# Twenty weight folds as ten units of 32x32 TensorE tiles, and two gates moved within the last stage

## The chip, the cores and the metric

The kernel runs on one core of one Trainium2 chip. The metric is the device time of one execution in microseconds (us). The kernel before takes 2380.1 us, the median of three executions that lie between 2378.39 and 2380.84 us.

## What is computed

`x` is 2048 x 1024 float32. It is normalised by rows to `xn`. One branch is linear attention with 32 heads of 32 columns, the other a gated feed-forward layer of width 3584, and the output joins them:

```python
xn = layernorm(x)
q, k, v = heads(xn @ wqkv)                       # 32 heads of 32
pq, pk = q @ w_phi[h], k @ w_phi[h]              # 32x32 per head
phi(p) = concat(softmax(p), softmax(-p))
o = phi(pq) (phi(pk)^T v) / (phi(pq) . sum(phi(pk)) + 1e-6)
s = o @ wo
g = silu((silu(xn @ w1) * (xn @ w3)) @ w2)
out = x + s * g
```

Since `w_phi` acts on each head alone, the kernel folds it into the weights first: a column block of `wk` and of `wq` for one head is multiplied by that head's 32x32 matrix. These products are the folds that the change is about.

## The kernel before

**Stages.** Stage 1 computes `xn @ w1` and `xn @ w3` for 28 feature chunks `f` of 128 and two halves `tb` of the rows; each pair (tb, f) takes seven block products in the order of `ORDER` (names A11, A12, S2, S1, S3, S4, A22; index j = 0 to 6). Stage 2 makes keys, values and queries, stage 3 multiplies by `w2`, stage 4 (the last) does attention's last products and the output by 16 row tiles `t`. A product is written as a high and a low part with three passes (`PASSES`), so that one of the seven is twelve 128x128 by 512 products on TensorE. The entries of `events` are called steps here; step k is one call `gate_up(k)`. Step 52 is (tb 0, f 7, j 3), step 175 is (0, 25, 0) and step 196 begins the second half.

**Order.** In stages 1, 3 and 4 every engine's instructions, and the transfers on SP's queue, stand in the order of the program (`in_order`). Each queue is served in that order: an instruction that waits holds all behind it. In one step the order is: loads of raw weights (`load_at`), what `before` lists, the twelve products, the next split of weights (`prep_at`, four steps ahead of their use: ScalarE casts the high part, line 92, VectorE subtracts the low part, line 93), the sums of a new chunk's raw weights (`sums_at`; lines 128 and 129), what `after` lists, and last the reading of the PSUM bank (`read`).

**What `read` does.** A11 (j 0): ScalarE copies bank b to `h0` (line 625). A12 (j 1): VectorE adds bank a to `h0` (627), ScalarE applies silu (631). S2 (j 2): ScalarE copies bank b to `u0` (633). S1 (j 3): ScalarE copies bank c to `u1` (639). S3, S4 and A22 follow on VectorE and ScalarE (641 to 653). A11, S2, S3 and A22 of a chunk add up in one bank b, so S3's products wait until the copy of line 633 has read what S2 left.

**Side work and its planner.** Other work is put between the steps: turning and splitting rows of `x` (`side_x`), folds (`side_fold`), sums and splits of key and value weights (`side_kv`, eight blocks), stores of operands (`side_store`), and in the second half `side_w`. Each VectorE piece asks `room(step, cost)` for the first step from `step` on whose planned cost stays at or under 2.55. The steps' own costs are in `base`: in steady state 1.22 at j 2, 3, 4 and 5, 1.22 or 1.83 by turns at j 0, and 1.83 at j 1 and 6. A `side_kv` block asks for three pieces of 1.22 (the sums, B11, B21) and five of 0.61 (T2, T1, T3, B22, T4), one after the other; its four raw blocks are loaded five steps ahead of the sums, and each split is stored two steps later (line 444). The pieces are planned in the order of the calls near line 535: `side_x`, `side_fold`, `side_kv`, `side_store`, `side_w`.

**Folds.** Twelve folds are done at the start. Each of the other twenty (`side_fold`) loads 256 KB of `wkT` or `wqT` into a buffer of the pool `xp` (tag x, 14 buffers), multiplies its four 128x128 blocks by block diagonals `bd` of `w_phi` (line 247) into a PSUM bank of tag tr, copies the bank back on ScalarE (line 500) and stores 256 KB (line 501). The folds stand at steps 67 to 171, and ask the planner for nothing.

**Pools.** `xp` (28 KB of each partition) and `bdp` (the 4 KB of `bd`) are closed at step 175, and the pool `spare` takes their 32 KB. At once `fetch` (line 164) issues the loads of two operands of the second half, `op1A11` and `op1A12`, four transfers of 512 KB each, into the two tiles of `spare`. A tile that takes the room of others waits until the last instruction that uses those is done. Splits take buffers of tag q, 11 in all; `h0`, `u0`, `u1` and `t2` take those of tag w, 5 in all. The raw weights of f 27 are loaded at step 178 (lines 256 and 257) and summed at step 183.

**Last stage.** `attend(t, c)` does 32 products in 64x32 tiles (line 1336), read by ScalarE and VectorE (1341, 1342); `out_half` does 24 products of 128x128 by 512 (1351). `gate(i, j)` applies silu to one row tile of the feed-forward output (line 1053). The last pair, i = 7, is row tiles 11 and 15.

Of the kernel before, what the change touches and what calls it, by code (L numbers as in the profile page):

```python
# [8 lines left out]
F = mybir.dt.float32  # L9
# [7 lines left out]
S, D, H, DH, FF = 2048, 1024, 32, 32, 3584  # L17
P = 128
NT = S // P
ND = D // P  # L20
NF = FF // P
G = 8
NKB = NF // 4
FOLDS = 12
# [5 lines left out]
def tile_kernel(ctx: ExitStack, tc: tile.TileContext, x, wkT, wqT, wv, wphi, wo, w1, w3, w2, out):  # L30
    nc = tc.nc
    open_pools = {}

    def pool(name, bufs, **kw):

        open_pools[name] = tc.tile_pool(name=name, bufs=bufs, reuse_waits="tile", **kw)
        return open_pools[name].__enter__()
# [29 lines left out]
    pairs = [(8 * (i // 4) + i % 4, 8 * (i // 4) + i % 4 + 4) for i in range(NT // 2)]  # L67

    dram = ctx.enter_context(tc.tile_pool(name="dram", bufs=1, space=DRAM))
# [3 lines left out]

    xo_d = [{n: dram.tile([P, 4, 2, 4, P], F, name=f"xo_d{tb}{n}") for n in ANAMES} for tb in range(2)]
    wkv_d = [{n: dram.tile([P, 2, 4, 512], F, name=f"wkv_d{c}{n}") for n in BNAMES} for c in range(3)]
    wk_d = [[dram.tile([P, 512], F, name=f"wk_d{c}_{k}") for k in range(ND)] for c in range(2)]
    wq_d = [[dram.tile([P, 512], F, name=f"wq_d{c}_{k}") for k in range(ND)] for c in range(2)]


    wo_d = [[dram.tile([P, 2, 512], F, name=f"wo_d{c}_{k}") for k in range(ND)] for c in range(2)]  # L80
# [63 lines left out]
    ps = pool("ps2", 2, space=PSUM)  # L144
    BANKS = {"a": 1, "b": 2, "c": 2}
# [27 lines left out]
    def blk(name):  # L173
        return xp.tile([P, 4, P], F, name=name, tag="x")

    def flat(t):
        return t.rearrange("p k t -> p (k t)")
# [4 lines left out]
    early_z = small.tile([P, 256 + PAD], F, name="early_z", bufs=1)[:, :256]  # L182
    bd = bdp.tile([P, G, P], F, name="bd")
# [31 lines left out]
    def turn(half):  # L215
        pt = ps.tile([P, 4, P], F, name="pt", tag="tr", bufs=3)
        for k in range(4):
            nc.tensor.transpose(pt[:, k, :], half[:, k * P:(k + 1) * P], ident)
        return pt
# [18 lines left out]
    def load_w(wT, dch, c, t=None):  # L238
        wr = blk("wr") if t is None else t
        nc.sync.dma_start(wr, wT[dch][:, 4 * c:4 * c + 4])  # L240
        return wr

    def fold(wr, c):

        pw = ps.tile([P, 4, P], F, name="pw", tag="tr", bufs=3)
        for g in range(4):
            nc.tensor.matmul(pw[:, g, :], wr[:, g], bd[:, 4 * c + g, :], start=True, stop=True)  # L247
        return pw

    folds = [(wkT, k, c, wk_d[c][k]) for c in range(2) for k in range(ND)]  # L250
    folds += [(wqT, k, c, wq_d[c][k]) for c in range(2) for k in range(ND)]

    def b_load(f):

# [32 lines left out]
        nc.sync.dma_start(r.rearrange("p u n -> p (u n)"), x[t * P:(t + 1) * P, :])  # L287
        xs.append([r[:, h] for h in range(2)])

    phi_raw = flat(blk("phi")[:, :2]).rearrange("p (g f) -> p g f", f=DH)  # L290
    nc.sync.dma_start(phi_raw, wphi)
    fold_rooms = [room_b[:, 4 + k] for k in range(4)]
    fold_rooms += [work.tile([P, 4, P], F, name="wr", tag="h1", bufs=2) for _ in range(2)]
# [19 lines left out]
    for j in range(4):  # L313
        sl = slice(32 * j, 32 * j + 32)
# [57 lines left out]
    before, after, rooms = {}, {}, []  # L372
# [6 lines left out]
    def at(step, f, d=after):  # L379
        d.setdefault(step, []).append(f)  # L380
# [6 lines left out]
    events = [(0, f, j) for f, j in FIRST_PAIR] + [(0, f, j) for f in range(2, NF) for j in range(7)]  # L387
# [40 lines left out]
    def room(step, cost):  # L428

        while base.get(step, 0) + took.get(step, 0) + cost > 2.55:  # L430
            step += 1
        took[step] = took.get(step, 0) + cost
        return step

    def store_quad(step, d, src, name, then=None):

        step = room(step, 2 * OP_US if then else OP_US)

        def f():
            t = qp.tile(list(src().shape[:1]) + [2] + list(src().shape[1:]), R, name=name, tag="q")  # L440
            split(t[:, 0], t[:, 1], src())
            if then:
                then()
            at(step + 2, lambda: nc.sync.dma_start(d, t.bitcast(F)))
        at(step, f)
        return step

    def side_x(i, s0):
        xt, a, mv, sd, pts = [], {}, [], [], {}
        t0, t1 = pairs[i]  # L450

        def load():
            xt.extend(load_x(t, [flat(blk("xt")) for _ in range(2)]) for t in (t0, t1))
            mv.append(small.tile([P, 2, 2], F, name="mv", bufs=4))

        at(s0, load)
        at_ = s0 + 2
        for j in range(2):
            at_ = room(at_ + 1, 1.3)
            at(at_, lambda j=j: stats(mv[0], j, xt[j]))  # L460
        at_ = room(at_ + 1, 1.0)
        at(at_, lambda: sd.append(list(rstd(mv[0]))[1]))
        for j in range(2):
            at_ = room(at_ + 1, 1.0)
            at(at_, lambda j=j: norm(mv[0], sd[0], j, xt[j]))
        s1 = at_ + 1
        for m, (n, j, hf) in enumerate((("A11", 0, 0), ("A12", 0, 1), ("A21", 1, 0), ("A22", 1, 1))):
            at(s1 + m, lambda n=n, j=j, hf=hf: pts.update({n: turn(xt[j][hf])}), before)
            at(s1 + m, lambda n=n: a.update({n: raw_x(pts[n])}))
        at_ = s1  # L470
        for n in ("A11", "A12"):
            at_ = store_quad(at_ + 1, xo_d[1][n][:, i - 4], lambda n=n: a[n], f"xo{n}")
        at_ = max(at_, s1 + 6)
        for m in range(3):
            at_ = room(at_ + 1, OP_US if m else 2 * OP_US)
            at(at_, lambda m=m: a_sums(a, nc.vector, m))
        for n in ("S3", "S1", "S2", "S4", "A22"):
            at_ = store_quad(at_ + 1, xo_d[1][n][:, i - 4], lambda n=n: a[n], f"xo{n}")

    def side_kv(c, k, s0):  # L480
# [8 lines left out]
        for n in BNAMES:  # L489
# [2 lines left out]
                    "B21": lambda: nc.vector.tensor_sub(r[1], r[1], t2[0])}.get(n)  # L492
            at_ = store_quad(at_ + 1, wkv_d[1 + c][n][:, :, k], lambda src=src: (r + t2)[src], "wkvo", then)

    def side_fold(m, s0):
        wT, k, c, d = folds[m]
        w = []
        at(s0, lambda: w.append(load_w(wT, k, c)))
        at(s0 + 5, lambda: w.append(flat(fold(w[0], c))), before)
        at(s0 + 5, lambda: nc.scalar.copy(flat(w[0]), w[1]))  # L500
        at(s0 + 7, lambda: nc.sync.dma_start(d, flat(w[0])))

    free = {2: HALF + 14}

# [29 lines left out]
    FIRST_STEP = 14  # L534
    for i in range(4, 8):
        side_x(i, FIRST_STEP + 13 * (i - 4))
    for m in range(FOLDS, len(folds)):
        side_fold(m, FIRST_STEP + 48 + 11 * (m - FOLDS) // 2)
    for m in range(8):
        side_kv(m // 4, m % 4, FIRST_STEP + 59 + 11 * m)  # L540
    for m in range(28):
# [3 lines left out]
    for u in range(2 * NKB):  # L545
        f = 4 * (u // 2) + 2 * (u % 2)
        units.append(([w2[(f + h) * P:(f + h + 1) * P, n * 512:(n + 1) * 512] for n in range(2) for h in range(2)],
                      lambda n, u=u: w2_d[u // 2][n][:, u % 2]))
    for k in range(4):
        units.insert(4 * k + 3, ([wq_d[n][k + 4 * h] for n in range(2) for h in range(2)],  # L550
                                 lambda n, k=k: wkv_d[0][n][:, :, k]))
# [16 lines left out]
    banks, parts = {}, {}  # L568
# [108 lines left out]
    _, sd = rstd(mvs[0], sds[0])  # L677
# [300 lines left out]
    ps = pool("ps", 2, space=PSUM)  # L978
    BANKS = {"a": 2, "b": 3, "c": 2}
    pend = None  # L980
    ready, ahead = [], {}
# [69 lines left out]
    def gate(i, j):  # L1051
        m, t = 2 * i + j, pairs[i][j]
        nc.scalar.activation(slabs[:, m], slabs[:, m], AF.Silu)
        if i < KEPT:
            nc.scalar.dma_start(g_d[t], slabs[:, m])
        else:
            gs[t] = slabs[:, m]
# [4 lines left out]
    def strips():  # L1062
        for a in range(2):
            for s in range(2):
                yield a, s, slice(64 * a + 32 * s, 64 * a + 32 * s + 32)
# [98 lines left out]
    def load_e(t):  # L1164
        for a, s, sl in strips():
            if t:
                m = e_at(t)
                nc.sync.dma_start(slabs[sl, m:m + 2].rearrange("i c (g n) -> i c g n", g=2), e_part(t, a, s))
            else:
                for c in range(2):  # L1170
                    nc.sync.dma_start(halves(e0[c][sl]), e_part(0, a, s)[:, c])
# [65 lines left out]
    for n in range(2 * EARLY):  # L1237
        at_ = 7 * 18 + 21 * n
# [13 lines left out]
    old, banks, first, second = None, {}, ready[0], None  # L1252
    in_order(ENG.SP, ENG.PE, ENG.Activation, ENG.DVE, ENG.Pool)
    for r, new in enumerate(steps):
# [29 lines left out]
        for m, (b, an, bn) in enumerate(TURN):  # L1284
# [13 lines left out]
            if i + 1 == len(pairs) and an in FIRST:  # L1298
                n = BNAMES.index(bn)
# [9 lines left out]
        old, banks = new, bank  # L1309
# [5 lines left out]
    ps = pool("ps4", 3, space=PSUM)  # L1315
# [50 lines left out]
    load_g(0)  # L1366
    for c in range(2):
        attend(0, c)()
    for j in range(2):
        gate(len(pairs) - 1, j)  # L1370
    prev = None
    for t in range(NT):
        p, last = out_half(t, 0), t + 1 == NT
        if t + 4 < NT:
            load_e(t + 4)
        if not last:
            for c in range(2):
                scale(t + 1, c)
        if t + 2 >= EARLY:
            weigh(t + 2)  # L1380
        if not last:
            for c in range(2):
                turn_e(t + 1, c)
        if t + 3 >= EARLY:
            z_products(t + 3)
        if prev:
            gated(t - 1, 1, prev, False)
            store_out(t - 1, 1)
        load_g(t + 1)
        gated(t, 0, p, last)  # L1390
        store_out(t, 0)
        if t + 2 >= EARLY:
            add_pairs(t + 2)
            invert(t + 2)
            factors(t + 2)
        lows = [attend(t + 1, 0)]
        prev = out_half(t, 1, lambda: lows.append(attend(t + 1, 1)))
        for c in range(2):
            if not last:
                lows[c]()  # L1400
            if t + 3 >= EARLY:
                z_sums(t + 3, c)
# [42 lines left out]
```

## Time and profile before

| what | value |
|---|---|
| median of three executions | 2380.1 us |
| the profiled execution's own time | 2381.62 us |
| its span in the trace | 2379.8 us |
| granted TensorE clock, mean | 0.999 |
| VectorE busy | 1760.9 us, 74% |
| ScalarE busy | 910.1 us, 38% |
| bytes moved | 578.00 MB, 243 GB/s |

The time of an execution exceeds the span of its trace by 1.8 us. In the views, PE is TensorE, PEld its weight loads, DVE VectorE, ACT ScalarE, POOL GpSimd, and SPq the sequencer of SP that issues transfers. A row of a timeline gives start, duration, engine, line, operation, tiles and count, and in brackets the idle time before it and what ended that. A row of the chain gives start, duration and what set the end. The program's float32 products appear as two records each.

### The profile page before, as it was taken

The page shows a single profiled execution, that of the slowest core. Times are in us where ns is not written, and L with a number is a line of the kernel's source. Part 1 is how long each engine was busy: PE and PEld are TensorE (multiplying, and loading weights), DVE is VectorE, ACT ScalarE, POOL GpSimd, SP SyncE. Part 2 cuts the span into 40 slices and gives each one's busy share as a digit, 9 for nine tenths or more (in the row PEclk, how much of TensorE's full clock was granted, in tenths as well). Part 3 has the DMA queues.
Part 4 walks back from the last instruction along what each step waited for, and adds up shares of the span by engine and source line. Part 5 has one row for each costly group of instructions (what it writes and reads, how often), then busy time and mean ns, then how long its engine had stood idle before and what let it go on. Part 6 is the DMA issues. An engine that isn't in the chain of part 4 may idle for free.

```text
span 2379.8 us, 37194 instructions
## 1 busy us (share of the span) xinstructions
PE 2351.0 (99%) x14348; PEld 1934.9 (81%) x14348; DVE 1760.9 (74%) x2729; ACT 910.1 (38%) x1597; POOL 257.6 (11%) x243
## 2 busy tenths in 40 slices
PE   7999999999999999999999999999999999999999
PEld 6788888888888888888788888887888888887887
DVE  8877788765688888875566666777678888786775
ACT  6445454543444554543212222334433333352000
POOL 1000000000000000000000000331012222213562
PEclk9999999999999999999999999999999999999999
DMA  5446699985998888865977878986435653478763
GB/s 215 146 155 212 230 354 332 328 266 186 289 303 283 292 306 289 268 209 195 384 287 277 306 253 307 364 315 249 159 124 151 204 177 133 156 245 272 213 179 103
DMA packets 291472, 578.00 MB, mean 243 GB/s; under 512 B 24912, under 2 KB 140768, under 8 KB 288608
## 3 DMA queue, kind: packets, MB, share of 16 engines
q1 hardware_dynamic: 284960, 552.56, 68.5%
q10 hardware_dynamic: 6336, 23.07, 2.5%
q8 instruction: 113, 1.85, 0.3%
q14 instruction: 63, 0.52, 0.1%
HBM read 372.64 MB, written 202.91 MB: 242 GB/s over the span
## 4 chain that ended last, share of the span: by engine, by line
PE 93%; DVE 3%; DMA 2%; ACT 1%; SPq 1%; issue 0%; POOL 0%; DVEq 0%; ACTq 0%; POOLq 0%
PE bankb L598 24%; PE bankb L1199 13%; PE bankc L598 12%; PE pm L1351 8%; PE bankb L794 7%; PE bankc L1199 6%; PE banka L598 6%; PE bankc L794 3%; PE banka L1199 3%; PE bankb L861 3%; PE banka L794 2%; PE bankc L861 1%; PE po L1336 1%; PE pkv L779 1%; PE pw L247 1%; PE banka L861 1%
## 5 line engine op out<-in xcount | busy, mean ns | idle before, releaser
L93 DVE TENSOR_TENSOR bo<-rw,bo 128x512 fp32r<-128x512 f32 x336 | 230.9, 689 | 158.2 <-ACT bo L92 155.4
L1199 PE MATMUL bankb<-bo,as 128*128 128x512 f32 x960 | 235.2, 389 | 1.2 <-ACT acc L1205 1.2
L1199 PEld LDWEIGHTS bankb<-bo,as 128*128 128x128 f32 x960 | 180.2, 188 | 39.0 <-ACT acc L1205 1.6
L92 ACT CAST bo<-rw 128x512 fp32r<-128x512 f32 x336 | 206.5, 617 | 13.8 <-DMA w_d2B<-w2o 3.4
L598 PE MATMUL bankb<-op0S,bo 128*128 128x512 f32 x672 | 164.6, 394 | 1.9 <-ACT op0S L92 1.2
L598 PE MATMUL bankc<-op0S,bo 128*128 128x512 f32 x672 | 162.2, 391 | 0.0
L1351 PE MATMUL pm<-wos,oT 128*128 128x512 f32 x672 | 161.1, 394 | 0.9 <-DVE oT L1342 0.9
L598 PE MATMUL bankb<-op1S,bo 128*128 128x512 f32 x672 | 161.4, 389 | 0.6 <-ACT u L633 0.6
L598 PE MATMUL bankc<-op1S,bo 128*128 128x512 f32 x672 | 161.2, 389 | 0.0
L598 PE MATMUL bankb<-op0A,bo 128*128 128x512 f32 x672 | 159.7, 391 | 0.8 <-DVE bo L93 0.5
L771 POOL MEMSET ev<- 128x32 f32 x32 | 4.1, 129 | 1427.1 <-DMA xoA<-xo_d0A 1073.2
L1199 PE MATMUL bankc<-bo,as 128*128 128x512 f32 x624 | 158.4, 389 | 0.0
L598 PE MATMUL bankb<-op1A,bo 128*128 128x512 f32 x672 | 157.6, 390 | 0.0
L598 PEld LDWEIGHTS bankb<-op0S,bo 128*128 128x128 f32 x672 | 126.3, 190 | 29.0 <-ACT op0S L92 1.6
L1351 PEld LDWEIGHTS pm<-wos,oT 128*128 128x128 f32 x672 | 124.7, 188 | 29.5 <-DVE oT L1342 1.7
L598 PEld LDWEIGHTS bankb<-op1A,bo 128*128 128x128 f32 x672 | 125.9, 188 | 27.4 <-DVE u L641 1.3
L598 PEld LDWEIGHTS bankb<-op1S,bo 128*128 128x128 f32 x672 | 126.1, 188 | 27.1 <-ACT u L633 1.0
L598 PEld LDWEIGHTS bankc<-op1S,bo 128*128 128x128 f32 x672 | 126.1, 188 | 26.2
L598 PEld LDWEIGHTS bankb<-op0A,bo 128*128 128x128 f32 x672 | 125.2, 188 | 26.9 <-DVE bo L93 0.8
L598 PEld LDWEIGHTS bankc<-op0S,bo 128*128 128x128 f32 x672 | 125.4, 188 | 25.6
L1199 PEld LDWEIGHTS bankc<-bo,as 128*128 128x128 f32 x624 | 117.2, 188 | 24.4
L1213 DVE TENSOR_TENSOR acc<-bankb,acc 128x512 f32<-128x512 f32 x152 | 102.0, 685 | 31.1 <-PE bankb L1199 31.1
(262 smaller groups left out, 4343.8 us busy)
## 6 DMA issues: line engine op xcount, KB each, us to landing
rw<-in_w SPq DMA_DIRECT2D x112, 512.0 KB, 4.4
hr<-h_d SPq DMA_DIRECT2D x56, 512.0 KB, 4.8
h_d<-h SPq DMA_DIRECT2D x111, 256.0 KB, 5.4
xoS<-xo_d0S SPq DMA_DIRECT2D x44, 512.0 KB, 6.2
xoS<-xo_d1S SPq DMA_DIRECT2D x44, 512.0 KB, 6.1
xoA<-xo_d0A SPq DMA_DIRECT2D x33, 512.0 KB, 4.9
xoA<-xo_d1A SPq DMA_DIRECT2D x33, 512.0 KB, 4.4
e_d<-eq ACTq DMA_DIRECT2D x32, 512.0 KB, 6.3
```

Of the source, the lines that this page charges most:

```text
L92: nc.scalar.copy(hi, src)
L93: (by or nc.vector).tensor_sub(lo, src, hi.bitcast(F))
L247: nc.tensor.matmul(pw[:, g, :], wr[:, g], bd[:, 4 * c + g, :], start=True, stop=True)
L598: nc.tensor.matmul(bank[b], bos[tb, f][bn][:, w, k], ao[an][:, u, k], start=first and n == 0, stop=LAST[b] == an and n == 11, skip_group_c ...
L771: nc.gpsimd.memset(v[:, :, DH:], 1.0)
L779: nc.tensor.matmul(pkv[sl, m], e[:, m // 4, (m % 4) * P + 32 * h:(m % 4) * P + 32 * h + 32], v[:, 4 * (m % 4) + h], start=first and m == 0 ...
L794: nc.tensor.matmul(bank[b], xo[an][:, u, k], wb[bn][:, w, k], start=an in ("A11", "A12", "S1") and n == 0, stop=LAST[b] == an and n == 11, ...
L861: nc.tensor.matmul(bank[b], xo[an][:, u, k], wb[bn][:, w, k], start=an in ("A11", "A12", "S1") and n == 0, stop=LAST[b] == an and n == 11, ...
L1199: nc.tensor.matmul(bank[b], t[:, u, pos + k], bos[kb, bn, k][:, w], start=first and n == 0, stop=LAST[b] == an and n == 5, skip_group_chec ...
L1213: nc.vector.tensor_add(c, pb, c)
L1336: nc.tensor.matmul(po[32 * j:32 * j + 32, a, 64 * k:64 * k + 64], kvs[sl, j, c, k], et[sl, :, 4 * k + j], start=True, stop=True, skip_grou ...
L1351: nc.tensor.matmul(p, oTs[t, h][:, a, k], wos[c, 4 * h + k][:, b], start=n == 0, stop=n == 3 * ND - 1)
```

## The change

The twenty later folds become ten units. A unit loads its weights into the room of `bd` (free after the first twelve folds), multiplies in 32x32 tiles with `w_phi` itself as the weights (it now lies in `early_z` until the last stage needs that tile), and turns the product back with 32x32 transposes on VectorE, into the same room. Units 0 and 1 do the last four `wk` blocks, in two head groups each; units 2 to 9 do one head group of `wq` over all eight blocks. The tiles of row group j write bank j: three banks of tag tr and bank a. The transposes ask the planner for 0.7 twice per unit. The next unit's load stands at least two steps behind the store of the one before. The input `wqT` gets a layout of contiguous 4 KB rows. In the last stage the two gates of pair 7 move from ahead of the loop into the loop's second and third row tile.

```diff
-    wk_d = [[dram.tile([P, 512], F, name=f"wk_d{c}_{k}") for k in range(ND)] for c in range(2)]
-    wq_d = [[dram.tile([P, 512], F, name=f"wq_d{c}_{k}") for k in range(ND)] for c in range(2)]
+    wk_d = [[dram.tile([P, 512], F, name=f"wk_d{c}_{k}") for k in range(ND if c == 0 else 4)] for c in range(2)]
+    wk_late = dram.tile([4, P, 512], F, name="wk_late")
+    wk_d[1] += [wk_late[k] for k in range(4)]
+    wq_all = [dram.tile([ND, P, 512], F, name=f"wq_d{c}") for c in range(2)]
+    wq_d = [[wq_all[c][k] for k in range(ND)] for c in range(2)]
...
-    phi_raw = flat(blk("phi")[:, :2]).rearrange("p (g f) -> p g f", f=DH)
+    phi_raw = early_z.rearrange("p (g f) -> p g f", f=DH)
...
     def side_fold(m, s0):
-        wT, k, c, d = folds[m]
-        w = []
-        at(s0, lambda: w.append(load_w(wT, k, c)))
-        at(s0 + 5, lambda: w.append(flat(fold(w[0], c))), before)
-        at(s0 + 5, lambda: nc.scalar.copy(flat(w[0]), w[1]))
-        at(s0 + 7, lambda: nc.sync.dma_start(d, flat(w[0])))
+        assert 2 < events[s0][2] < 6
+        w, banks = [flat(bd)], []
+        if m < 2:
+            gs_, nd = (4 + 2 * m, 5 + 2 * m), 4
+        else:
+            gs_, nd = (m - 2,), ND
...
+        def multiply():
+            banks.extend(ps.tile([P, 512], F, name="pf", tag="tr", bufs=3) for _ in range(3))
+            banks.append(ps.tile([P, 512], F, name="banka", bufs=BANKS["a"]))
+            for n, g in enumerate(gs_):
+                wn = w[0][:, 512 * n:512 * n + P * nd].rearrange("p (d k) -> p d k", d=nd)
+                for q in range(4):
+                    for j in (3, 0, 1, 2):
+                        sl = slice(32 * j, 32 * j + 32)
+                        nc.tensor.matmul(banks[j][32 * q:32 * q + 32, P * n:P * n + 32 * nd], phi_raw[sl, g], wn[sl, :, 32 * q:32 * q + 32],
+                                         start=True, stop=True, skip_group_check=True)
...
+        def turn(j):
+            for n in range(len(gs_)):
+                o = w[0].rearrange("p (d n f) -> p d n f", d=nd, f=DH)[:, :, 4 * n + j]
+                nc.vector.transpose(o, banks[j][:, P * n:P * n + 32 * nd].rearrange("p (d f) -> p d f", f=DH))
...
+        ready = max(s0 - 5, fold_free[0])
+        assert ready <= s0 - 3, (m, ready, s0)
+        at(ready, load)
+        at(s0, multiply, before)
+        at_ = s0 - 1
+        for js in ((3, 0), (1, 2)):
+            at_ = room(at_ + 1, 0.7)
+            for j in js:
+                at(at_, lambda j=j: turn(j))
+        at(at_ + 2, store)
+        fold_free[0] = at_ + 4
...
-    for m in range(FOLDS, len(folds)):
-        side_fold(m, FIRST_STEP + 48 + 11 * (m - FOLDS) // 2)
+    for m, s0 in enumerate((52, 66, 87, 96, 108, 117, 129, 138, 150, 159)):
+        side_fold(m, s0)
...
-    for j in range(2):
-        gate(len(pairs) - 1, j)
     prev = None
     for t in range(NT):
         p, last = out_half(t, 0), t + 1 == NT
         if t + 4 < NT:
             load_e(t + 4)
+        if 0 < t < 3:
+            gate(len(pairs) - 1, t - 1)
...
-        "wqT": lay(wqkv[:, :D]),
+        "wqT": wqkv[:, :D].T.reshape(G, P, D),
```

More of the change, by code (lines that the diff above doesn't have):

```diff
@@ L248, in fold @@
         return pw
-    folds = [(wkT, k, c, wk_d[c][k]) for c in range(2) for k in range(ND)]
-    folds += [(wqT, k, c, wq_d[c][k]) for c in range(2) for k in range(ND)]
+    folds = [(wkT, k, c, wk_d[c][k]) for c in range(2) for k in range(ND)][:FOLDS]
     def b_load(f):
@@ L493, in side_kv, with load, store @@
             at_ = store_quad(at_ + 1, wkv_d[1 + c][n][:, :, k], lambda src=src: (r + t2)[src], "wkvo", then)
+    fold_free = [0]
     def side_fold(m, s0):
-        wT, k, c, d = folds[m]
-        w = []
-        at(s0, lambda: w.append(load_w(wT, k, c)))
-        at(s0 + 5, lambda: w.append(flat(fold(w[0], c))), before)
-        at(s0 + 5, lambda: nc.scalar.copy(flat(w[0]), w[1]))
-        at(s0 + 7, lambda: nc.sync.dma_start(d, flat(w[0])))
+        assert 2 < events[s0][2] < 6
[4 more added lines that the diff above has]
+            gs_, nd = (m - 2,), ND
+        def load():
+            if m < 2:
+                for n, g in enumerate(gs_):
+                    nc.sync.dma_start(w[0][:, 512 * n:512 * n + 512].rearrange("p (d n) -> p d n", d=4),
+                                      wkT[4:, :, g].rearrange("d p n -> p d n"))
+            else:
+                nc.sync.dma_start(w[0], wqT[gs_[0]])
+        def multiply():
+            banks.extend(ps.tile([P, 512], F, name="pf", tag="tr", bufs=3) for _ in range(3))
+            banks.append(ps.tile([P, 512], F, name="banka", bufs=BANKS["a"]))
+            for n, g in enumerate(gs_):
+                wn = w[0][:, 512 * n:512 * n + P * nd].rearrange("p (d k) -> p d k", d=nd)
[8 more added lines that the diff above has]
+                nc.vector.transpose(o, banks[j][:, P * n:P * n + 32 * nd].rearrange("p (d f) -> p d f", f=DH))
+        def store():
+            if m < 2:
+                d = wk_late.rearrange("d p n -> p d n")[:, :, 256 * m:256 * m + 256]
+            else:
+                d = wq_all[gs_[0] // 4].rearrange("d p n -> p d n")[:, :, P * (gs_[0] % 4):P * (gs_[0] % 4) + P]
+            nc.sync.dma_start(d, w[0].rearrange("p (d n) -> p d n", d=nd))
+            banks.clear()
+        ready = max(s0 - 5, fold_free[0])
[9 more added lines that the diff above has]
+        fold_free[0] = at_ + 4
```

## The prediction

> **What bounds the kernel now.** I read the page's busy times first, then the chain of waits in stage 1, where the folds are.
>
> ```profile
> PE 2351.0 (99%) x14348; PEld 1934.9 (81%) x14348; DVE 1760.9 (74%) x2729; ACT 910.1 (38%) x1597; POOL 257.6 (11%) x243
> ```
>
> ```profile
> 229.69 0.89 PE pw L247 x8
> 230.58 2.74 PE bankb L598 x12
> ...
> 506.33 2.72 PE banka L598 x12
> 509.05 2.72 PE bankb L598 x12
> ...
> 531.72 0.89 PE pw L247 x8
> 532.61 2.74 PE bankc L598 x12
> ...
> 557.10 2.72 PE bankc L598 x12
> ```
>
> TensorE is busy for 99% of the span, and from 190 to 560 us the chain is TensorE alone: a step of twelve products takes 2.72 us, a fold 0.89 us, and the step behind it 2.74. So a fold costs 0.91 us of the end, and nothing else is late there. The other engines and the queue have slack, VectorE least of all:
>
> ```profile
> 300.00:360.00 60.00, 60.00 (x283) 50.26 (x282) 48.82 (x77) 31.74 (x60) 0.00 (x0) 1.00 0.99 347
> 360.00:420.00 60.00, 60.00 (x278) 50.15 (x277) 48.00 (x75) 30.13 (x57) 0.00 (x0) 1.00 1.00 338
> ```
>
> By windows of 60 us, the columns are length, PE, PEld, DVE, ACT and POOL busy, clock, DMA share and GB/s. VectorE is busy for 48 to 49 of 60, and the DMA engines always.
>
> **The folds.** Removed are 20 x 0.91 = 18.2 us of TensorE, all on the path. The trace has no 32x32 tiles. The nearest row is the last stage's 32 products in 64x32 tiles:
>
> ```profile
> 2183.87 2.72 PE pm L1351 x12
> 2186.59 0.79 PE po L1336 x53
> 2187.38 2.98 PE pm L1351 x12
> ```
>
> Such a group costs 0.79 us and makes the next twelve products 0.26 longer (2.98 against 2.72): 1.05 us in all. In it each of eight tiles streams four products of 64 columns, 256 columns. A unit has the same 256 columns for each of its sixteen tiles (one product of 256, or two of 128). If all sixteen run side by side it costs the same 1.05 us, ten units 10.5 us, and the gain is 7.7 us. From the fold row, 128 columns take 0.89/4 = 0.22 us, so 256 take 0.45, and 0.60 of the 1.05 is filling and changing. If eight tiles run at a time, a unit costs 0.90 + 0.60 = 1.50 and the gain is 3.2; if four, 1.8 + 0.6 = 2.4 and 5.8 are lost. Below, no unit can be under 0.45, a gain of 13.7. I take 1.05, since the 64x32 row shows eight tiles side by side.
>
> **Emptying the banks.** Twenty copies leave ScalarE, and VectorE gets 48 transposes from PSUM, 32 of 256 columns and 16 of 128.
>
> ```profile
> L500 ACT COPY wr<-pw x20: 569/588/593, 232.3 to 532.8; 128x512 f32<-128x512 f32 x20
> ```
>
> ```profile
> L1179 DVE STREAM_TRANSPOSE acc<-acc 128x1024 f32<-128x1024 f32 x30 | 35.5, 1220 | 0.0
> L964 DVE TENSOR_TENSOR s<-hr,sm 128x256 f32<-128x256 f32 x56 | 23.4, 418 | 0.0
> ```
>
> A transpose of 256 columns lies between a quarter of the 1220 ns row, 0.31 us, and the 256-column row, 0.42; I take 0.4, and 0.3 for 128 columns: 18 us in all over some 300 us, 3.6 in a window of 60 where VectorE has 11 idle. ScalarE's 0.59 x 20 was hidden and its removal gains nothing. Without VectorE's idle time the transposes would cost 18 us.
> [...]
>
> **Transfers of the units.** Bytes are the same. The one tight place is a single room for load, product and store. Unit 3 loads at step 93, two steps behind unit 2's store, and multiplies at 96.
>
> ```profile
> rw<-in_w SPq DMA_DIRECT2D x36, 512.0 KB, 5.1
> ...
> xo_d0S<-op0S SPq DMA_DIRECT2D x16, 512.0 KB, 7.4
> ```
>
> Store and load need 7.4 + 5.1 = 12.5 us of the 13.6 in five steps; if both take 7.4, TensorE waits 1.2. I take 0.5. All other units have six steps or more.
>
> **What the transposes move in the plan.** This is the term that decides. A step may hold 2.55. A unit's two pieces of 0.7 take, from step 87 on, two steps that have 1.22 of their own; what is left there, 0.63, still takes a 0.61 piece but no 1.22 piece. A key/value block needs three pieces of 1.22, which fit only in these steps, and is planned after the units. Walking `room` for both kernels gives the sums of the eight blocks at steps 81, 96, 107, 115, 123, 135, 143, 156 before, and 81, 107, 121, 131, 142, 152, 164, 172 after. The last block's splits stood at 157 to 163; they now stand at 173 (B11) and 175 to 180 (B21, T2, T1, T3, B22, T4). The walk agrees with the trace of before: step 163 begins at 509.05, and VectorE does that block's T4 at 512.55:
>
> ```profile
> 512.55 0.69 DVE L93 TENSOR_TENSOR wkvo<-wkv,wkvo 128x512 fp32r<-128x512 f32 x1
> ```
>
> But `xp`, which holds the block's raw weights, is closed at step 175, and there SP's queue reaches the first load into `spare`. It must wait for the last reader of the room. That such a wait holds the queue is to be seen already before, where it was a fold's store:
>
> ```profile
> SPq L164 <- DMA wq_d<-wr: 4.4, 1, 4.4
> ```
>
> ```profile
> 538.12 11.90 SPq L164 DMA_DIRECT2D op1A<-xo_d1A  x8
> 550.11 2.27 SPq L556 DMA_DIRECT2D h_d<-h  x1
> 552.47 0.69 SPq L256 DMA_DIRECT2D rw<-in_w  x1
> 553.22 0.45 SPq L257 DMA_DIRECT2D rw<-in_w  x1
> ```
>
> Now the reader is T4's subtraction at step 180. In the clock of before that step begins at 557.10 (a shift by what the units gained moves all alike). T4 ends 512.55 + 0.69 - 509.05 = 4.2 us into its step: 561.3. (Its buffer of tag q comes no sooner: seven unstored splits and four weights of TensorE fill all 11, so it waits for step 180's products, to 559.8.) Queued behind are the eight loads, two splits' stores, a store of h and, at step 178, the raw weights of f 27.
>
> Before, these landed 553.22 + 5.1 - 538.12 = 20.2 us behind the first load. 1.9 of that was a wait of the h store for VectorE, which falls away:
>
> ```profile
> SPq L556 <- DVE bo L93: 1.9, 1, 1.9
> ```
>
> The two splits' stores add 2 x 11.90/8 = 3.0. So they land at 561.3 + 20.2 - 1.9 + 3.0 = 582.6. VectorE wants them at step 183:
>
> ```profile
> 567.05 0.68 DVE L128 TENSOR_TENSOR rw<-rw 128x512 f32<-128x512 f32 x1
> 567.77 0.69 DVE L129 TENSOR_TENSOR t<-rw 128x512 f32<-128x512 f32 x1
> ```
>
> ```profile
> 569.10 0.63 ACT L631 ACTIVATE h<-h 128x512 f32<-128x512 f32 x1 [2.69 <-DVE h L627]
> 569.63 0.60 ACT L92 CAST bo<-rw 128x512 fp32r<-128x512 f32 x1
> 570.74 0.59 ACT L633 COPY u<-bankb 128x512 f32<-128x512 f32 x1 [0.50 <-PE bankb L598]
> ```
>
> ```profile
> 573.42 2.72 PE bankb L598 x12
> ```
>
> Behind these sums in VectorE's order stands A12's add (0.68), behind that ScalarE's silu (0.63), a cast (0.60) and the copy of u0 (0.59), and for that copy S3's products of step 186 wait. 582.6 + 0.68 + 0.69 + 0.68 + 0.63 + 0.60 + 0.59 = 586.5, where step 186 began at 573.42: TensorE stands for 13.1 us. After it nothing is late: f 27's first products come three steps on.
>
> **The gates.** Two activations leave ScalarE's queue ahead of the loop, and come back in the loop.
>
> ```profile
> 2167.05 2.01 ACT L1053 ACTIVATE acc<-acc 128x1024 f32<-128x1024 f32 x2
> 2173.18 0.59 ACT L1341 CAST oT<-po 128x512 fp32r<-128x512 f32 x1 [4.12 <-PE po L1336]
> ...
> 2187.50 0.59 ACT L1341 CAST oT<-po 128x512 fp32r<-128x512 f32 x1 [9.95 <-PE po L1336]
> ```
>
> ScalarE idles 4.12 us behind them in the old place and 9.95 in the new, and their results are used only at tiles 11 and 15: 0. Without cover it would be 1 us each way. Moving `phi` into `early_z` and the layouts cost nothing on any engine.
>
> **Sum.** -18.2 + 10.5 + 0.5 + 13.1 = +5.9 us. On the profiled execution of 2381.6 that gives 2387.5; it lies 1.5 above the median of 2380.1, from which I count: 2386.
>
> **Rivals.** *The queue's hold reaches no one* (not slower). If the raw weights of f 27 land by 573 or so, the cover is enough. The slack is 567.05 - 558.3 = 8.7 us at VectorE and some 2 at TensorE. For it: in the trace VectorE's order is all that ties them, and a release earlier than I read it would do; the point is a hold that ends before some 551 instead of 561.3. Against it: the 4.4 us wait shows that line 164 does wait for the old users. Then the time is 2380.1 - 7.7 + 0.5 = 2373.
>
> *Half a hold.* If the readers lie only under the second tile of `spare`, the first four loads go out at their old place and the weights land 4 x 1.49 = 6.0 us sooner: a stall of 7.1, a sum of -0.1, 2380. For it: buffers are given out in turn, so five of fourteen can lie on one side. Against: four raw blocks go out together and T4's alone is enough for the full hold.
>
> *The tiles don't run side by side* (the change doesn't do what it says). With four at a time units cost 24 us: 2380.1 + 5.8 + 0.5 + 13.1 = 2400. The 64x32 row speaks against it; that its eight tiles use two row groups, not four, for it.
>
> **How the numbers follow.** The forecast has 0.53, no hold 0.18, half a hold 0.19, slow tiles 0.10. What this measurement can tell from no change is about 0.2%, 4.8 us: 2375.3 to 2384.9. The forecast's own range, with units of 1.05 to 1.5, a load wait of 0 to 1.2 and 3 us either way on the landing, is 2382 to 2394; about a quarter of it is under 2384.9. Faster: no hold, and a little of the half hold where units are cheaper, 0.20. Same: 0.17 of the half hold and 0.13 of the forecast, 0.30. Slower: 0.50. The range reaches down to no hold with units a little cheaper, 2371, and up to 2394, and leaves out slow tiles and the ends.
>
> **What would show it.** Right: in place of line 247's pieces the chain has ten groups of 32x32 products of about 0.8 us; the key/value splits end near step 180; the SP waits name line 164 with a VectorE split as releaser, some 20 us long; VectorE's sums of f 27 wait for the raw weights; and TensorE has one gap of about 13 us ahead of a bank b step near 565 us. Wrong: no gap there; or units over 1.5 us; or gaps at the units' loads instead; or any gap in the last stage's first three tiles.

## The result and the profile after

The changed kernel takes 2392.6 us (median of four executions, 2389.62 to 2393.69) against 2379.2 for the kernel before on the same chip: a ratio of 1.0053, interval 1.0036 to 1.0071, or 12.6 us more (8.6 to 16.9). The time is inside the range, and slower as forecast; the forecast had +5.9 us. The execution profiled is the fastest of the four, 2389.62 us, with a span of 2387.8.

The page of the changed kernel: busy times, and the slices of the granted clock.

```profile
PE 2345.8 (98%) x14572; PEld 1922.2 (81%) x14572; DVE 1773.2 (74%) x2777; ACT 899.2 (38%) x1577; POOL 256.6 (11%) x243
...
PEclk9999999998999999999999999999999999999999
```

TensorE does 5.2 us less work than before, 2345.8 against 2351.0, in a span that is 8.0 longer: it stands still somewhere. The one 8 among the clock's slices is the tenth, 537 to 597 us, and points to the place.

**The units.** The chain of waits around the third unit; columns start, duration, and what set the end.

```profile
284.72 2.72 PE bankb L647 x12
287.44 0.33 PE banka L524
...
288.08 2.94 PE bankc L647 x12
```

The sixteen products of 256 columns take 288.08 - 287.44 = 0.64 us, and the twelve behind them 0.22 more than 2.72: 0.86 for a unit of `wq`, of which there are eight. The first two units, with 32 products of 128 columns, take longer:

```profile
185.89 0.22 PE banka L524
...
186.89 2.96 PE bankc L647 x12
```

1.00 and 0.24. All ten cost 8 x 0.86 + 2 x 1.24 = 9.4 us, so the gain on the folds is 18.2 - 9.4 = 8.8. The 48 transposes, grouped by the tile that they read, are about as long as taken: 0.41 to 0.44 us for 256 columns and 0.27 for 128 (ns least, median and most, then first and last start):

```profile
L530 DVE STREAM_TRANSPOSE bd<-banka x12: 273/442/445, 195.5 to 491.8; 128x256 f32<-128x256 f32 x8, 128x128 f32<-128x128 f32 x4
L530 DVE STREAM_TRANSPOSE bd<-pf x36: 270/407/444, 195.9 to 495.9; 128x256 f32<-128x256 f32 x24, 128x128 f32<-128x128 f32 x12
```

**The hold.** The chain from 547 to 586 us:

```profile
547.94 2.73 PE bankc L647 x12
...
550.75 0.63 ACT wkvo L95
...
551.40 0.70 DVE wkvo L96
...
552.12 0.38 SPq L167
...
563.00 1.46 SPq L446
...
566.22 1.35 SPq L258
...
567.62 7.06 DMA rw<-in_w
...
574.70 0.70 DVE rw L131
...
575.42 0.69 DVE t L132
...
577.89 0.49 ACT u L682
...
578.42 4.65 PE bankb L647 x12
583.07 2.75 PE bankc L647 x12
```

Read backwards: the bank b products of step 186 wait for the copy of `u0` (now line 682), this for VectorE's sums of f 27 (131 and 132), these for its raw weights, whose loads (258) stand behind a store of h (605, not shown), two splits' stores (446) and the loads into `spare` (167), and these wait for the last split of the last key/value block (96). The waits, of SP's queue and of all engines, confirm both ends:

```profile
SPq L167 <- DVE wkvo L96: 24.3, 1, 24.3
```

```profile
DVE rw L131 <- DMA rw<-in_w: 14.5, 1, 14.5
PE bankb L647 <- ACT u L682: 14.2, 1, 14.2
```

TensorE stands for 14.2 us, and the twelve products behind take 4.65 us in place of 2.72. The windows show why (length, busy times of PE, PEld, DVE, ACT and POOL, granted clock, DMA share, GB/s):

```profile
560.00:570.00 10.00, 4.25 (x19) 3.19 (x17) 0.20 (x1) 0.00 (x0) 0.00 (x0) 0.91 1.08 337
570.00:580.00 10.00, 1.57 (x4) 1.30 (x5) 3.72 (x6) 3.25 (x7) 0.00 (x0) 0.50 1.04 385
580.00:590.00 10.00, 10.00 (x42) 8.15 (x41) 5.71 (x10) 2.10 (x4) 0.00 (x0) 0.90 0.50 175
```

The granted clock is 0.50 in the window in which TensorE comes back, 0.90 in the next and 1.00 from 590 us on. The twelve products lose 4.65 - 2.72 = 1.9 us by it. The hold costs 14.2 + 1.9 = 16.1 us.

**A gap that was not foreseen.** TensorE's timeline at the start of the last stage (idle time and releaser in brackets), and the chain there:

```profile
2170.64 1.71 PE L1385 MATMUL po<-acc,kvs 64*32 64x64 f32 x128
2175.06 6.64 PE L1400 MATMUL pm<-wos,oT 128*128 128x512 f32 x21 [2.71 <-DMA wos<-wo_d]
```

```profile
2168.26 6.62 DMA wos<-wo_d
2174.87 0.19 issue
2175.06 7.32 PE pm L1400 x24
```

Before, these 24 products followed without a pause and took 5.83 us:

```profile
2164.89 1.64 PE po L1336 x106
2166.53 5.83 PE pm L1351 x24
```

So 2.7 + 1.5 = 4.2 us are lost here. The named releaser, a load of `wos`, is not the cause. Of all loads, the first of these products waits by the program for the first of the fourteen of `wos` alone, and the trace has that one landed at 2103.6, some 71 us earlier; the first cast of `oT`, its other wait, is done at 2172.1. The load that the chain names is a later one on the same semaphore, and its last part lands at 2176.4, when the products have already begun. What makes the gap was a question for the experiments.

**The balance.** -8.8 + 16.1 + 4.2 = +11.5 us, and the medians differ by 12.6 (8.6 to 16.9). The spans of the two profiled executions differ by 8.0 only, since these two differ in small waits elsewhere too. Three that the one of before has and the one of after lacks come to 2.7 us:

```profile
650.16 2.12 PE L598 MATMUL bankb<-op1S,bo 128*128 128x512 f32 x8 [0.58 <-ACT u L633]
1613.83 3.04 PE L861 MATMUL bankb<-op4T,xoS 128*128 128x512 f32 x12 [1.16 <-ACT q L867]
2181.29 4.62 PE L1351 MATMUL pm<-wos,oT 128*128 128x512 f32 x19 [0.93 <-DVE oT L1342]
```

The other way, in the one of after twelve products of stage 2 take 4.58 us, where the same row of before has 3.00:

```profile
1161.92 4.58 PE L843 MATMUL bankb<-op2T,xoA 128*128 128x512 f32 x12 [1.75 <-DMA xoA<-xo_d0A]
```

So the spans bear out the terms to some 2 us, no better. Such waits differ between the two traces: the gap of 1.75 us there is 1.50 in the one of before.

### The profile page after: what moved, and what is told of

It is laid out like the page before. It is cut to its first block, busy times and chain, and to the rows that moved or that the text cites. A ratio compares the mean times of both kernels' runs of the same rounds, so it can differ in the third digit from the quotient of the medians.

```text
span 2387.8 us, 37599 instructions
## 1 busy us (share of the span) xinstructions
PE 2345.8 (98%) x14572; PEld 1922.2 (81%) x14572; DVE 1773.2 (74%) x2777; ACT 899.2 (38%) x1577; POOL 256.6 (11%) x243
## 3 DMA queue, kind: packets, MB, share of 16 engines
q8 instruction: 115, 1.88, 0.3%
## 4 chain that ended last, share of the span: by engine, by line
PE 94%; DMA 2%; DVE 2%; SPq 1%; ACT 1%; issue 0%; POOL 0%; DVEq 0%; ACTq 0%
PE bankb L647 24%; PE bankb L1248 13%; PE bankc L647 12%; PE pm L1400 8%; PE bankb L843 7%; PE bankc L1248 6%; PE banka L647 6%; PE bankb L910 4%; PE bankc L843 3%; PE banka L1248 3%; PE bankc L910 2%; PE banka L843 2%; PE po L1385 1%; PE banka L910 1%; PE pkv L828 1%; DMA xoA<-xo_d0A 1%
## 5 line engine op out<-in xcount | busy, mean ns | idle before, releaser
L647 PE MATMUL bankb<-op0S,bo 128*128 128x512 f32 x672 | 164.1, 393 | 16.1 <-ACT u L682 14.2
```

Of the source, the lines that this page charges most:

```text
L647: nc.tensor.matmul(bank[b], bos[tb, f][bn][:, w, k], ao[an][:, u, k], start=first and n == 0, stop=LAST[b] == an and n == 11, skip_group_c ...
```

## The experiments

The theory: the units save what the trace says, and the planner's room for the transposes pushes the last key/value block past the closing of `xp`, which holds SP's queue. Its rivals: the planner has no part in it and the units' own work is late; or the gates, or something else at the start of the last stage, make the loss. A further theory came with the first results: the loading of TensorE's own instructions makes the gap in the last stage. Line numbers are those of the changed kernel unless it says otherwise. Each ratio is to the kernel before on the same chip.

### Closing the pools later

The pools close at step 182 in place of 175, behind the last split of step 180.

```diff
-        if f == NF - 3 and j == 0:
+        if (f, j) == (NF - 2 if tb == 0 else NF - 3, 0):
```

> The changed kernel, with xp and bdp closed and the two loads into spare issued at step 182 instead of 175. Theory (the queue's hold): SP no longer waits for the last key/value split, the raw weights of f 27 land in time, and the gap of 14.2 us at step 186 goes, with the 1.9 us that the slow products behind it took. Left is the gain of the units, 18.2 - 9.4 = 8.8 us: about 2370.4. Rival A (VectorE's 48 transposes make it late): the gap stays, 2390 or more. Rival B (the units' transfers in 512-byte pieces crowd the raw weights): the gap shrinks by a part only, 2380 to 2388.

2376.4 us, ratio 0.9983 (0.9974 to 0.9992): 4.0 us faster than before, some 16.6 faster than the changed kernel. The steps from 558 to 597 us run without a gap (step 186 begins at 564.30), and the queue's wait for the split is 1.2 us:

```profile
564.30 2.88 PE L647 MATMUL bankb<-op0S,bo 128*128 128x512 f32 x12
```

```profile
SPq L167 <- DVE wkvo L96: 1.2, 1, 1.2
```

So the hold is what cost most. But the 2370.4 that was expected, the full gain of the units, did not appear: the last stage keeps its gap, and the 24 products take 7.35 again.

```profile
2161.43 6.67 PE L1400 MATMUL pm<-wos,oT 128*128 128x512 f32 x21 [2.80 <-DMA wos<-wo_d]
```

### The transposes without room in the plan

```diff
-            at_ = room(at_ + 1, 0.7)
+            at_ += 1
```

> The changed kernel, with the transposes put at s0 and s0 + 1 without asking the planner, so that the eight key/value blocks get the steps of before (last split at 163). Theory (the plan moved the last block past the close): no hold beyond the few us of before, 2370 to 2372. Rival A (VectorE is late by its transposes): unplanned pieces crowd VectorE still more, TensorE waits at many units, 2385 or more. Rival B (transfers): about as the changed kernel, 2388 to 2393, since they are the same.

2377.0 us, 0.9986 (0.9977 to 0.9995). The pools close as early as in the changed kernel, every unit still turns its banks on VectorE, and no gap stands near 564 us: the last split of a key/value block begins at 506.19, far ahead of the closing.

```profile
506.19 0.69 DVE L96 TENSOR_TENSOR wkvo<-wkv,wkvo 128x512 fp32r<-128x512 f32 x1
```

So the transposes themselves hold nobody; their entries in the plan do. The time is some 5 us above the 2370 to 2372 expected; the last stage's gap, here 3.46 us, is still there.

### The plan's entries alone, in the kernel before

Put ahead of the loop over `side_kv` in the kernel before; the folds stay, and nothing is transposed.

```diff
+    for s0 in (52, 66, 87, 96, 108, 117, 129, 138, 150, 159):
+        at_ = s0 - 1
+        for _ in range(2):
+            at_ = room(at_ + 1, 0.7)
```

> The kernel before with its folds as they were, but with the planner's room taken at the steps where the units take it (two times 0.7 each), so that the last key/value block ends at step 180 as in the changed kernel. No work is added. Theory (hold): the same gap as in the changed kernel, 14 us and 2 us of slow products: 2379.2 + 16 = 2395. Rivals A and B: no transposes and no new transfers, so 2379 as before.

1.0054 (1.0041 to 1.0068): 12.9 us slower than before, with no instruction added and none removed. The profiled execution, 2392.29 us, shows the hold in the timelines of VectorE, SP and TensorE (lines of the kernel before, moved by 4 from the new loop on):

```profile
556.95 0.68 DVE L93 TENSOR_TENSOR wkvo<-wkv,wkvo 128x512 fp32r<-128x512 f32 x1
```

```profile
557.66 10.16 SPq L164 DMA_DIRECT2D op1A<-xo_d1A  x8
```

```profile
582.77 5.45 PE L602 MATMUL bankb<-op0S,bo 128*128 128x512 f32 x12 [9.29 <-ACT u L637]
```

9.3 us idle and 2.7 on the twelve products behind (5.45 for 2.72) are 12.0. This settles the cause of the hold: reservations that move other work are enough for it. It is shorter than in the changed kernel: the loads go out right behind a split that ends at 557.63, one ahead of the block's last, which begins at 560.63 here. Why they do not wait for the last one too was not tried.

### The raw weights of f 27 first

The pools close at step 178, and the loads into `spare` stand right behind those of f 27's raw weights in the queue.

```diff
-        if f == NF - 3 and j == 0:
+        for late in load_at.get(step, ()):
+            rws.append(b_load(late[1]))
+        if (f, j) == (NF - 3, 3 if tb == 0 else 0):
...
-        for late in load_at.get(step, ()):
-            rws.append(b_load(late[1]))
```

> The changed kernel, with the pools closed at step 178, just behind the issue of the raw weights of f 27 in SP's queue. SP is still held until the split at step 180, some 8 us. Theory (it is the place of the raw weights behind the hold that costs, not the hold itself): no gap at step 186, about 2370.4 as with the late close. Rival (the hold itself, or the 4 MB of loads into spare, slows what follows): a gap of 3 us or more stays.

2376.6 us, 0.9986 (0.9977 to 0.9994). The loads into `spare` still wait 6.0 us for the split, and TensorE does not stand near 564 us:

```profile
SPq L167 <- DVE wkvo L96: 6.0, 1, 6.0
```

So no cost of the wait as such shows; what costs is that the raw weights of f 27 stand behind it. The gap in the last stage is 4.05 us.

### The gates back at their old place

The kernel with the late closing, and the two gates ahead of the last stage's loop.

```diff
+    for j in range(2):
+        gate(len(pairs) - 1, j)
...
-        if 0 < t < 3:
-            gate(len(pairs) - 1, t - 1)
```

> The changed kernel with the late close, and the two gates of pair 7 back at their old place ahead of the loop. In the late close's trace a gap of 2.8 us stands ahead of the last stage's first 128x128 products, which the kernel before doesn't have. Theory P (TensorE's own instructions come late: a load of 16 KB of them ends just ahead of the gap's end, and the folds' rewrite has moved the place in the program where such a load falls): the gates are ScalarE's and move nothing on TensorE, so the gap stays and the time is that of the late close, 0.9983 of before. Rival G (the gates' move makes the gap): it goes, 2371 to 2372, 0.9964.

2376.4 us, 0.9982 (0.9973 to 0.9991), the same as with the gates moved; the gap is 3.26 us. No worth of the gates shows in either place (each interval is some 2 us either way), and they do not make the gap.

### 128 more instructions ahead of everything

The kernel with the late closing, and in stage 0, behind `first_copies(1)`, 32 products whose result nothing reads.

```diff
+    pad = ps.tile([P, 4, P], F, name="pad", tag="tr", bufs=3)
+    for k in range(32):
+        q = 32 * (k % 4)
+        nc.tensor.matmul(pad[q:q + 32, 0, :32], bd[:32, 0, :32], bd[:32, 0, :32], start=True, stop=True,
+                         skip_group_check=True)
```

The theory of the instruction load rests on the profiles' pages. Queue q8 carries instructions (packets, MB, share): 113 loads before, 115 after.

```profile
q8 instruction: 115, 1.88, 0.3%
```

1.88 MB / 115 is 16 KB, and 2 x 14572 instructions of TensorE (products and weight loads) / 115 is 253; before, 2 x 14348 / 113 is 254. Taking q8 as TensorE's, and with its waits counted in, I put a load at 256 instructions, an estimate. The last stage's first two groups in 64x32 tiles, x128 in the timeline above, are 256 instructions with their weight loads, one whole load, and they pass in 1.71 us, where 256 instructions of twelve-product steps take some 29 (24 in 2.72 us). Counted in the built programs, the first of these 256 stands at place 0 within a load in the kernel before, at 193 in the changed one, and at 64 with the 128 more. The count includes waits that stand as instructions of their own, one more or fewer from kernel to kernel, so the places can differ by one from the sum; anything that may stand ahead of the program is not in it, so only the differences say something.

> The changed kernel with the late close, and 32 products in 32x32 tiles put into TensorE's first wait, whose result nothing reads. They move the rest of TensorE's program by 128 instructions, half of a 16 KB load. Theory P: the gap of 2.8 us in the last stage goes, with the slow products behind it: some 4 us under the late close, 2371 to 2373, 0.9964. Rival (the gap comes from the loads of wo, which are as they were): the gap stays, 0.9983.

2370.8 us, 0.9963 (0.9950 to 0.9975): 8.8 us faster than before (5.9 to 11.9), the units' whole gain. It is the fastest version found. TensorE goes through the place without a pause:

```profile
2159.07 1.71 PE L1390 MATMUL po<-acc,kvs 64*32 64x64 f32 x128
2160.72 5.24 PE L1405 MATMUL pm<-wos,oT 128*128 128x512 f32 x21
```

### The same in the kernel before

48 such products (192 instructions, and one wait more) bring the kernel before to the changed one's place.

```diff
+    for k in range(48):
+        q = 32 * (k % 4)
+        nc.tensor.matmul(pad[q:q + 32, 0, :32], bd[:32, 0, :32], bd[:32, 0, :32], start=True, stop=True,
+                         skip_group_check=True)
```

> The kernel before, with 48 such products in the same wait, so that the last stage's first 64x32 group begins at the same place within 16 KB as in the changed kernel (instruction 193 of 256 in both, against 0 before). Nothing else is changed. Theory P: a gap of 2 to 4 us appears ahead of the last stage's first 128x128 products, and the time is some 4 us longer, 1.0017. Rivals: as before, 1.0000.

2384.4 us, 1.0015 (1.0006 to 1.0024), 3.6 us slower than before, and the gap is there:

```profile
2168.63 6.65 PE L1356 MATMUL pm<-wos,oT 128*128 128x512 f32 x21 [2.94 <-DMA wos<-wo_d]
```

Neither units nor moved gates are needed for it. It also gives the units' gain a second time: with the gap in both kernels, 2384.4 here and 2376.4 with the gates back differ by 8.0 us, on one chip.

### 256 more instructions

The kernel with the late closing again, with 64 such products: one whole load, so that all behind stands at its place without them. The other lines are as above.

```diff
...
+    for k in range(64):
...
```

> The kernel with the late closing and 64 such products in place of 32: 256 instructions, one whole load, so that everything behind them stands at the same place within its load as without them. If the place of the 64x32 products within a load decides, the gap of 2.8 to 3.3 us ahead of the last stage's first 128x128 products is back, and the ratio is that of the kernel without such products plus some 1 us for the 64: 0.998 to 0.999 (2376 to 2378 us). If the extra products help in another way (TensorE's clock, a shift of the loads in time), it stays near 0.996 (2371 to 2372 us) without a gap.

2377.3 us, 0.9985 (0.9976 to 0.9994), and the gap is back:

```profile
2160.74 7.89 PE L1405 MATMUL pm<-wos,oT 128*128 128x512 f32 x21 [4.17 <-DMA wos<-wo_d]
```

So it is not the extra products that help but where the 256 instructions stand within a load. The queues in the two microseconds from 2158 to 2160 of this kernel, in the middle of that gap:

```profile
q8 instruction: 1, 0.02, 3.0%
```

From 2150 to 2158 there is no such packet.

### The changed kernel with 128 more instructions

The early closing is kept, and the 32 products are added to the changed kernel as it is.

> The changed kernel with its early closing of the raw-weight pools kept, and 32 products on a 32x32 corner (128 instructions of TensorE) put into stage 0. If the hold of the queue and the late instruction load are two costs that add, only the second goes: the ratio to the kernel before is 1.0053 - 0.0019 to 0.0023 = 1.003 (2386 to 2388 us), TensorE keeps one gap of 12 to 15 us near 564 us, and none ahead of the last stage's first 128x128 products. If the gap in the last stage was a consequence of the hold or only of the closing, the ratio stays at 1.005.

2389.6 us, 1.0035 (1.0022 to 1.0047), or 8.3 us more than before (5.2 to 11.2). The gap in the last stage is gone, the hold is not:

```profile
580.46 5.10 PE L647 MATMUL bankb<-op0S,bo 128*128 128x512 f32 x12 [14.52 <-ACT u L682]
```

```profile
2174.88 1.71 PE L1390 MATMUL po<-acc,kvs 64*32 64x64 f32 x128
2176.52 5.20 PE L1405 MATMUL pm<-wos,oT 128*128 128x512 f32 x21
```

-8.8 for the units and 14.5 + 2.4 for the hold make +8.1; the median lies 1.6 us above the 2386 to 2388 expected, with a hold that is 0.8 longer than in the trace of the changed kernel. Here the instruction packet passes at 2158 to 2160, some 15 us ahead of the 64x32 products; in the changed kernel it passes at 2172 to 2174, inside the gap of 2172.35 to 2175.06. The two losses are separate and add.

### The order of the tiles

The kernel with the late closing and the 32 products, its units multiplied row group by row group.

```diff
-                for q in range(4):
-                    for j in (3, 0, 1, 2):
+                for j in (3, 0, 1, 2):
+                    for q in range(4):
```

> The padded kernel, with the two inner loops of a unit's products exchanged: the four column groups of one row group come one after the other, instead of the four row groups. If the sixteen tiles run side by side whatever the order, a unit of wq costs 0.87 us as in the changed kernel and the time is that of the padded one. If products of one row group share a path into the array, such a unit costs 1.3 us or more and the time is 4 us longer.

2372.3 us, 0.9966 (0.9953 to 0.9978). A unit takes 288.45 - 287.81 = 0.64 us, as in the other order, and 2.94 behind it:

```profile
287.81 0.35 PE banka L524 x4
...
288.45 2.94 PE bankc L647 x12
```

Two rounds of 256 columns would take 2 x 0.45 = 0.90 us by the fold's row, so the sixteen tiles run side by side, in either order.

## Why the prediction was right, and where its sum was short

**What bounds the kernel:** right. With hold and gap gone, the units' 8.8 us appear in full in the time.

**The units:** the mechanism was right, 10.5 us was 1.1 too much. The price from the 64x32 row, 1.05, lies between the two kinds: 0.86 with one product of 256 columns for each tile, 1.24 with two of 128. That the two cost the same was the wrong part. The 128-column form issues twice the products; that this is why it is dearer is argued, not tried. The fill and change that I put at 0.60 of 1.05 is 0.86 - 0.45 = 0.41 in the first form.

**Emptying the banks:** right, 0.41 to 0.44 and 0.27 us, hidden. VectorE is busy for 46 to 51 of 60 us in the windows from 180 to 540 us, TensorE for all of each.

**Transfers of the units:** 0.5 was predicted, and nothing was lost: TensorE has no idle time from 180 to 540 us. The issues of the units (KB each, us to landing) stay under the 13.6 that unit 3 has:

```profile
bd<-in_wqT SPq DMA_DIRECT2D x8, 512.0 KB, 4.8
wq_d<-bd SPq DMA_DIRECT2D x8, 512.0 KB, 6.8
```

**The plan and the queue:** right link by link. The last split ends 552.10 - 547.94 = 4.2 us into step 180, as predicted; the raw weights land 574.68 - 552.12 = 22.6 us behind the first load, where 21.3 were predicted (the transfer took 7.06 and not 5.1); from there to the products it is 3.7 for 3.9. The gap is 14.2 for 13.1.

**What failed is the sentence "After it nothing is late".** No engine was late, but TensorE's clock was, at 0.50 in the window of its return: 1.9 us on the first twelve products, not in the sum.

**The gates:** no worth shows, as predicted. Yet the prediction called any gap in the last stage's first three tiles a proof against it. There is one, ahead of the first, and the gates do not make it; 4.2 us for this gap is the term that the sum did not have. The part on the change counted products and never how the 256 instructions of the 64x32 groups stand in the program.

**In numbers:** the hold 16.1 for 13.1, the gap 4.2 for 0, the load wait 0 for 0.5, the units 9.4 for 10.5: 3.0 + 4.2 - 0.5 - 1.1 = 5.6 above the forecast's 5.9, so 11.5, inside the measured 8.6 to 16.9. That the time still fell inside the range, 1.4 us under its upper end, is in part luck: that end was drawn for dearer units and a later landing, and what filled it is mostly the gap and the clock, which were not in the sum.

**The rivals:** without a hold the time was put at 2373; with the late closing it is 2376.4, and 2370.8 where the gap in the last stage is gone too. Half a hold is not what came: the queue waits at the first of the eight loads, so all of them wait. Slow tiles are refuted by 0.64 us for a unit.

## What to carry to other kernels

A planner's entry can cost even where its work is hidden: follow what it pushes back until that piece's last reader is compared with the point at which its room is given away, and keep loads that are wanted soon ahead of any load that waits for room. To a stall like the 14.2 us here add what the products behind it lose: 1.9 us, at a granted clock of 0.50. Where a kernel passes through a hundred tiny products in a row, as here, a change anywhere before them shifts their place in the instruction stream; in these runs that cost 3.6 us (48 products more in the kernel before) or brought 5.6 (32 more behind the late closing). So look for a gap there before explaining a small difference.

## What the runs showed of the hardware

**A gap came and went with the place in the instruction stream.** Where the 256 instructions of 1.71 us stand at one place within a load, as counted above, TensorE stands 2.7 to 4.2 us behind them (six kernels and the changed one); where they stand some 63 places further (the kernel before) or some 128 (with the 32 products), it does not. The program's own waits do not account for the gap, as told for the changed kernel, and an instruction packet passes inside it in the two kernels for which that is shown. The runs show that the place decides; that the gap is a wait for that load is my reading, and how it comes about is not shown. Why the gap varies was not tried.

**The clock dropped after short gaps too, though not after each.** Behind gaps of 2.71 and 2.80 us the 24 products took 7.32 and 7.35 in place of 5.83, and the window behind the latter shows 0.75:

```profile
2160.00:2165.00 5.00, 3.57 (x11) 2.85 (x12) 4.52 (x4) 0.00 (x0) 0.00 (x0) 0.75 1.02 416
```

The length of the gap alone does not decide. Behind the 1.75 us in stage 2 of the changed kernel, shown above, the granted clock was 0.78 and 0.80 in the two windows of 4 us from 1160 on; behind 3.56 us at the start of the same trace it was 1.00:

```profile
14.42 5.37 PE L221 MATMUL pt<-ident,xt 128*128 128x128 f32 x28 [3.56 <-DVE xt L216]
```

```profile
12.00:15.00 3.00, 0.58 (x3) 0.59 (x4) 2.43 (x10) 1.80 (x4) 0.00 (x0) 1.00 1.02 418
15.00:20.00 5.00, 4.78 (x27) 4.54 (x25) 4.50 (x10) 3.63 (x7) 0.00 (x0) 1.00 1.03 411
```

What decides was not tried.
